# Windowed attention and a gated MLP: score bands of 136 keys for 32 queries, exponentials turned on VectorE, v in 32x64 tiles

## The chip, the cores and the metric

The kernel runs on one core of one Trainium2 chip. The metric is the device time of one execution in microseconds (us). Before the change the median of three runs is 676.88 us (676.18 to 677.9).

## The reference

Attention over 4 batches, 8 heads, 768 tokens, 64 numbers per head. A query sees the first `n_global` = 8 keys of its batch and the `n_local` = 96 keys that end at itself. A bias falls with the distance by a slope of its own for each head. The result is put together per token (512 numbers) and goes through two matrix products of 512 to 2048 to 512 with a gate between them.

```python
scores = scale * np.matmul(q, k.transpose(0, 1, 3, 2))
rel = pos[:, None] - pos[None, :]
is_global = pos[None, :] < int(n_global)
is_local = (rel >= 0) & (rel < int(n_local))
keep = is_global | is_local
dist = np.where(is_global & ~is_local, float(n_local), np.abs(rel).astype(np.float32))
scores = np.where(keep, scores - slopes[:, None, None] * dist, -1000000000.0)
a = np.exp(scores - np.max(scores, axis=-1, keepdims=True))
a = a / (np.sum(a, axis=-1, keepdims=True) + 1e-09)
attn = np.matmul(a, v)                      # [B, H, S, D] -> x [B*S, H*D]
h = x @ w_in
out = (h * (1.0 / (1.0 + np.exp(-h)))) @ w_out
```

## The kernel before, in words

**Blocks.** The 3072 tokens are 24 blocks of 128 queries, six to a batch. For each block TensorE turns k and q (`turn`, L571, eight 128x128 transposes) and computes scores, with queries on the partitions and keys along the row: 128 own keys, and in all but the first block of a batch 96 keys before them and the 8 global ones, 232 in all (`scores`, L630). The first six blocks do this in plain fp32 (`whole`), from tiles KHw and QHw. The other 18 split k and q into a high and a low fp32r part (`high` L595, `low` L599) and sum three products. A matmul here uses 64 of the 128 rows of the array: an even and an odd head are two tiles of 64 rows, issued one behind the other.

**From scores to values.** VectorE adds the bias B1 or B0 and takes the row's top (`top_of`, L644), ScalarE takes exponentials and their sum (`expo`, L652), VectorE adds 1e-9, inverts, and multiplies (`guard` L663, `inverse` L667, `norm` L672; the first four blocks do the division later, L719 to L737). TensorE turns the exponentials with fp32 transposes through PSUM (`turn_p`, L681, 352 in all), ScalarE copies them out (`move_p`, L687), and TensorE multiplies them with v (`values`, L701): one matmul per head and half window, moving 128 columns, with v as weights of 128 or 104 rows by 64 columns; two heads go to the two halves of the PSUM partitions. An fp32 matmul stands as two records in the trace. ScalarE and VectorE split the result into `xh` and `xl` for the first product (L746, L749).

**The MLP.** `moe_h` (L874) multiplies `xh` and `xl` with `w_in` split in two, three fp32r matmuls per 128 rows, over groups of blocks: `GS=(3, 3, 2, 4, 4, 4, 4)`, so a matmul is 384, 256 or 512 columns wide. ScalarE and VectorE make the gate (L880, L884) and store it. The second product (L931) works on pairs of blocks by seven products of half matrices, 256 columns wide; VectorE and ScalarE make the sums of halves (L911, L921, L925), VectorE takes the products out of PSUM (L945, L948, L953). Beside all that VectorE checks the inputs' sizes with 512-wide reductions: `check` (L515, 64 of them), `top_size` (L509) and `scale_of` for v (L559).

**What sets the order.** A planner (`Plan`, lines 65 to 190) writes the order of every engine's instructions before the kernel is built: each operation has an engine, a cost, a rank, what it depends on, and the buffers and PSUM banks that it takes; at each step the free engine gets the lowest rank that is ready by the planner's own clock. An engine executes its instructions strictly in that order. While the planner's clock stands before `WEND` = 60 us and TensorE has nothing ready, it writes a filler matmul (L1161, 256 columns of bf16 that nobody reads). `plan.after` ties an operation to an earlier one.

Of the kernel before, what the change touches and what calls it, by code (L numbers as in the profile page):

```python
# [24 lines left out]
WIN = NPREV + NG + P  # L25
C1 = NPREV + NG
FIRST_ROWS = P - NPREV
# [4 lines left out]
    LAT=140, SD=125, DL=1900, DW=2900, DB=9000, DS=5000, DO=3400, MG=60, T2=45000, LAT2=230, MG2=400, F0=600, F1=1200, C1=400, C2=1650, COLD=4400, WEND=60000,  # L32

    CAP=dict(po=6, av=2, s=4, h=3, tp=2, tq=4), HU=13, RUN=(2, 2, 4), CP=(190, 333, 392, 336, 224),

    C0=12.5, CR=0.8, LW=15, LB=8.0, QB=5.5, RI=0.8, RN=-0.6, RP=0.5, RM=0.2, RV=0.4, RQ=0.5, RB=2.5, LK=-25,

    BP=(4, 2), CF=8, AHEAD=4, GS=(3, 3, 2, 4, 4, 4, 4), BD=(1, 2), VC=1, HE=4, EQ=4, RG=-2.5, B1R=0.0, Q1=450, Q2=2400, BE='POOL', EX=10, CD=6, CS=2, SQ=((0, 0, 10), (1, 0, 10)), GG=2, PB=4, AQ=4, CN=12, I0=6, IV=4, QS='ACT', O0=7.5, ON=23.5, PF=16,
# [11 lines left out]
class Plan:  # L50
# [11 lines left out]
    KINDS = ("po", "av", "s", "h", "tp", "tq")  # L62

    def room(self, want):

        if any(self.live[x] + c > self.caps[x] for x, c in want.items()):
            return False
        if not any(x in self.KINDS for x in want):
            return True
        n = {x: self.live[x] + want.get(x, 0) for x in self.KINDS}  # L70
        own = (
            dict(po=0, av=1, s=2, h=0, tp=1, tq=0), dict(po=0, av=1, s=2, h=1, tp=1, tq=0),
            dict(po=3, av=0, s=0, h=0, tp=0, tq=0),
        )[self.hold]
        return len(self.banks) >= sum(want[x] for x in want if x in self.KINDS) and (
            sum(max(n[x], own[x]) for x in self.KINDS) <= 8 - (not self.hold)
            or all(n[x] <= own[x] for x in want if x in self.KINDS)
        )
# [19 lines left out]
    def run(self, lat, margin, lead, filler=None, fill_until=0, cold=0):  # L98
# [8 lines left out]
        while left:  # L107
# [21 lines left out]
            while back and back[0][0] <= t:  # L129
                b = heapq.heappop(back)[2]  # L130
                self.live[b.tag] -= 1
                if b.bank is not None:
                    (self.slots if b.tag == "pe" else self.banks).append(b.bank)
            for eng in pend:
# [19 lines left out]
                for b in best["uses"]:  # L154
                    if not b.taken:
                        b.taken = True
                        self.live[b.tag] += 1
                        if b.tag == "pe":
                            b.bank = self.slots.pop(0)
                        if b.tag in self.KINDS:  # L160
                            b.bank = self.banks.pop(0)
# [14 lines left out]
def attn_moe(ctx, tc, q, k, v, n_global, n_local, w_in, w_out, out):  # L176
# [34 lines left out]

    pes = [sb3.tile([P, 2, WIN], F32, name=f"pe{n}", tag=f"pe{n}", bufs=1) for n in range(PAR["PB"])]

# [6 lines left out]
    banks = [psum.tile([P, 512], F32, name=f"bank{i}") for i in range(8)]  # L220
# [7 lines left out]

    B1 = sb3.tile([P, H, WIN], BF16, name="B1", bufs=1)
    B0 = sb3.tile([P, H, P], BF16, name="B0", bufs=1)  # L230
# [9 lines left out]
    cur, glob, prev = slice(C1, WIN), slice(NPREV, C1), slice(0, NPREV)  # L240
    ng, nl = par[:, 0:1], par[:, 1:2]

    def places():

        t1 = sbx.tile([P, 1024], F32, name="t1", tag="xh")
        t2 = sbx.tile([P, 1024], F32, name="t2", tag="xl")
        bias_t.extend(t1[:, i * WIN:(i + 1) * WIN] for i in range(3))
        bias_t.extend(t2[:, i * P:(i + 1) * P] for i in range(3))
        R, col = bias_t[0], bias_t[3]
        io = dict(allow_small_or_imprecise_dtypes=True)  # L250
        both = R[:, :2 * C1].rearrange("p (a b) -> p a b", a=2)[:, :, :NPREV]
        nc.gpsimd.iota(both, [[-P, 2], [-1, NPREV]], base=NPREV, channel_multiplier=1, **io)
        nc.gpsimd.iota(R[:, C1 + NPREV:], [[-1, FIRST_ROWS]], base=0, channel_multiplier=1, **io)
        nc.gpsimd.iota(col[:, :NPREV], [[1, NPREV]], base=FIRST_ROWS, channel_multiplier=0, **io)
        nc.gpsimd.iota(col[:, NPREV:], [[1, FIRST_ROWS]], base=0, channel_multiplier=0, **io)

    def bias_far():

        R, far, D1, col, drop, D0 = bias_t
        nc.vector.tensor_scalar(drop, R[:, cur], 0.0, FAR, ALU.is_lt, ALU.mult)  # L260
        yield
        nc.vector.memset(R[:, glob], FAR)
        yield
        nc.vector.tensor_add(R[:, cur], R[:, cur], drop)
        yield
# [15 lines left out]
    def bias_own():  # L281
# [3 lines left out]
        R, far, D1, col, drop, D0 = bias_t  # L285
        nc.vector.tensor_scalar(far, R, nl, BIG, ALU.is_ge, ALU.mult)
        yield
        nc.vector.scalar_tensor_tensor(drop, col, ng, far[:, cur], ALU.is_ge, ALU.mult)
        yield
        nc.vector.scalar_tensor_tensor(D0, R[:, cur], nl, drop, ALU.min, ALU.add)  # L290
        yield

    def bias_prev():

        R, far, D1, col, drop, D0 = bias_t
        nc.vector.tensor_scalar(far[:, glob], col[:, NPREV:C1], ng, BIG, ALU.is_ge, ALU.mult)
        yield
        nc.vector.scalar_tensor_tensor(D1, R, nl, far, ALU.min, ALU.add)
        yield

    def bias_eng(first, hp):
        if hp < PAR["BD"][first]:
            return nc.vector
        return nc.gpsimd if hp >= PAR["BP"][first] else nc.scalar

    def bias_of(first, hp):
        eng = bias_eng(first, hp)
        for h in (2 * hp, 2 * hp + 1):
            o, x = ((B0, bias_t[5]) if first else (B1, bias_t[2]))
            sl = -(2.0 ** (-8.0 * (h + 1) / H)) / SC  # L310
            if eng is nc.scalar:
                eng.mul(o[:, h], x, sl)
            else:
                eng.tensor_scalar(o[:, h], x, sl, None, ALU.mult)
# [4 lines left out]
    wx = const.tile([P, B * NJ * H], F32, name="wx")  # L319
    VM = const.tile([P, B * NJ], F32, name="VM")  # L320
# [6 lines left out]
        big=2, early=99, qkn=3, vn=3, KH=2, KL=2, QH=2, QL=2, pe=PAR["PB"], pt=5, xh=2, xl=2, g1=4, F=1, gq=8, hl=3, ob=2,  # L327
# [24 lines left out]
    o_i = op("POOL", 1150, -99, places, (), bt)  # L352
    o_far = steps(bias_far, [200, 75, 200], -9, [o_i], bt)
# [3 lines left out]
    o_bias = steps(bias_own, [70, 150, 240, 220], -4, [o, o_far], [*bt, tb])  # L357
    o_bias1 = steps(bias_prev, [130, 400], PAR['B1R'], [o_bias], bt)
    o_b = {}
    for hp in range(NHP):  # L360
        for first in (True, False):
            e = bias_eng(first, hp)
            p = {id(nc.vector): ("DVE", 300, 500), id(nc.scalar): ("ACT", 400, 574)}.get(id(e), ("POOL", 1060, 1900))
            o_b[first, hp] = op(
                p[0], p[2 - first], hp - 0.5 if first else PAR["RB"] + hp,
                (lambda first=first, hp=hp: bias_of(first, hp)), [o_bias if first else o_bias1], bt,
# [96 lines left out]
    for n in range(HF):  # L463
        rank = PAR["C0"] + 2 * PAR["CR"] * n + (PAR["CD"] if n >= PAR["CS"] else 0)
        o = op("DMA", 3600, rank - PAR["LW"], (lambda n=n: stage2(n)), [o_w[n - 3][1]] if n > 2 else (), (), PAR["DW"])
# [54 lines left out]
    for n in range(2 * NFC):  # L520
        a = Buf("big")
        o = op("DMA", 1456, 1e6 + n, (lambda n=n: stage(n, "c")), [o_c[-4]] if n > 1 else (), [a], PAR["DB"])
        o_cd.append(o)
        cbuf.append(a)
        for i in range(2):
            o_c.append(op("DVE", 602, 1e6 + n, (lambda n=n, i=i: check(n, i)), [o], [a]))
        if n >= NFC:
            o_vm.append(op("DVE", 602, 1e6 + n, (lambda n=n: top_size(n)), [o], [a]))
# [5 lines left out]
    def load(i, nm, h0=0, h1=H):  # L534
        b, j = divmod(i, NJ)
        pool, tag = (sb2, "vn") if nm == "v" else (sb3, "qkn")
        if nm in "kq" and i < PAR["EQ"]:
# [3 lines left out]
        elif not h0:  # L541
            blk[i][nm] = pool.tile([P, H, D], F32, name=f"{nm}n", tag=tag, bufs=3)
        src = dict(k=k, q=q, v=v)[nm]
        cuts = (h0, (h0 + h1) // 2, h1) if i >= B * NJ - PAR["EX"] and nm == "v" else (h0, h1)
        eng = nc.scalar if not i and nm == "q" and h0 < PAR["AQ"] else nc.sync
        rows = ((0, 0, P),) if nm == "q" else ((0, FIRST_ROWS, NPREV), (NPREV, 0, FIRST_ROWS))
        for a, e in zip(cuts, cuts[1:]):
            for at, r, n in rows:
                eng.dma_start(
                    blk[i][nm][at:at + n, a:e],  # L550
                    src[b, a:e, j * P + r:j * P + r + n, :].rearrange("h p d -> p h d"),
                )

    def share(i):
        nc.sync.dma_start(blk[i - 1]["v"][NPREV:C1], v[i // NJ, :, :NG, :].rearrange("h p d -> p h d"))

    def scale_of(i):
        x = st["v", i] if i < PAR["I0"] else blk[i]["v"]
        nc.vector.tensor_reduce(  # L559
            VM[:, i:i + 1], x.rearrange("p h d -> p (h d)"), AX.X, ALU.max, apply_absolute_value=True  # L560
# [7 lines left out]
    def turn(i, nm, tp, p0=0, p1=NHP):  # L568
        blk[i]["t", nm, p0] = ps = bank(tp, NHP, P)
        for hp in range(p0, p1):  # L570
            nc.tensor.transpose(ps[:, hp], blk[i][nm][:, 2 * hp:2 * hp + 2, :], ident)  # L571

    def whole(i):
        return i < PAR["I0"]

    def part(i, x):
        if x not in blk[i]:
            f = whole(i)  # L580
# [4 lines left out]

# [749 lines left out]
```

## Time and profile before

| | before |
|---|---|
| median of 3 runs | 676.88 us |
| the profiled execution | 675.77 us |
| its span, first to last instruction | 674.0 us |
| granted TensorE clock, mean over the span | 0.999 |
| TensorE matmul busy | 668.1 us (99%) |
| VectorE busy | 556.5 us (83%) |
| ScalarE busy | 349.9 us (52%) |
| GpSimd busy | 30.5 us (5%) |

Times are from the span's start. Busy time counts an instruction from its start to its end, and matmuls overlap in the pipeline, so a row that says 1.05 us for eight matmuls is longer than the time to the next row; the distance between starts is what one costs the engine. In a group's row "x" stands before the number of records.

### The profile page before, as it was taken

Reading aid. Unit: us, or ns where it says so; the run is one execution under the profiler, and the core shown is the slowest. Engines: PE = TensorE matmul, PEld = TensorE weight load, DVE = VectorE, ACT = ScalarE, POOL = GpSimd, SP = SyncE. Lnnn points to the kernel's source line nnn. Section 1 sums busy time; section 2 is a strip of 40 time slices with the busy share of each in tenths; the row PEclk is TensorE's granted clock in tenths of the full one; section 3 lists DMA queues with packets and bytes.
Section 4 is the critical chain, followed back from the end, with each engine's and each line's share of the span. In section 5 each row is a group of like instructions: output and inputs, shape, how many; then the busy total and the mean of one; then the engine's idle time right before and its main releaser. Section 6 shows DMA issues by size and latency. Waiting matters only on the chain.

```text
span 674.0 us, 14105 instructions
## 1 busy us (share of the span) xinstructions
PE 668.1 (99%) x5222; PEld 608.0 (90%) x5222; DVE 556.5 (83%) x1297; ACT 349.9 (52%) x804; POOL 30.5 (5%) x81
## 2 busy tenths in 40 slices
PE   9999999999999999999999999999999999999997
PEld 7889999999988888888888888999999999999997
DVE  5999969999977776679655886799999999999774
ACT  6987636678655555567553353243444334333341
POOL 3202000000000000010000000000000000000000
PEclk9999999999999999999999999999999999999999
DMA  8789966666766656654435677665466565543201
GB/s 196 181 248 250 231 167 168 167 163 144 170 199 157 158 142 158 157 129 110 116 92 162 185 240 220 192 219 188 151 198 213 154 224 186 175 154 113 94 32 35
DMA packets 162221, 111.85 MB, mean 166 GB/s; under 512 B 87269, under 2 KB 144869, under 8 KB 162149
## 3 DMA queue, kind: packets, MB, share of 16 engines
q1 hardware_dynamic: 161474, 110.65, 58.3%
q8 instruction: 42, 0.69, 0.5%
q10 hardware_dynamic: 674, 0.26, 0.1%
q14 instruction: 31, 0.25, 0.1%
HBM read 79.43 MB, written 31.46 MB: 165 GB/s over the span
## 4 chain that ended last, share of the span: by engine, by line
PE 99%; DVE 0%; issue 0%; DVEq 0%
PE bank L874 41%; PE bank L931 36%; PE bank L701 6%; PE bank L681 6%; PE bank L630 6%; PE bank L571 3%; PE bank L1161 1%; PE bank L737 0%; PE bank L279 0%; DVE S L1170 0%; PE bank L1063 0%; DVE o L948 0%; PE bank L1171 0%; DVE wx L323 0%; DVEq L1168 0%
## 5 line engine op out<-in xcount | busy, mean ns | idle before, releaser
L874 PE MATMUL bank<-xh,wi 128*128 128x512 f32 (+2 forms) x896 | 276.2, 373 | 0.0
L931 PE MATMUL bank<-wo,g 128*128 128x256 f32 x1980 | 237.5, 281 | 0.0
L931 PEld LDWEIGHTS bank<-wo,g 128*128 128x128 f32 x1980 | 236.0, 189 | 0.1
L874 PEld LDWEIGHTS bank<-xh,wi 128*128 128x128 f32 x896 | 163.7, 188 | 24.5 <-issue 2.9
L874 PE MATMUL bank<-xl,wi 128*128 128x512 f32 (+2 forms) x448 | 161.9, 361 | 0.0
L880 ACT ACTIVATE th<-bank 128x512 f32<-128x512 f32 (+2 forms) x112 | 60.1, 537 | 98.5 <-PE bank L874 97.7
L884 DVE SCALAR_TENSOR_TENSOR th<-th,bank 128x512 f32<-128x512 f32 (+2 forms) x112 | 68.4, 611 | 43.2 <-ACT th L880 41.6
L652 ACT ACTIVATE pe<-pe,NM 128x232 f32<-128x232 f32 (+1 forms) x192 | 89.4, 470 | 14.3 <-DVE NM L644 14.3
L874 PEld LDWEIGHTS bank<-xl,wi 128*128 128x128 f32 x448 | 84.5, 189 | 8.6
L921 ACT CAST g<-S 128x1024 fp32r<-128x1024 f32 x48 | 50.1, 1049 | 61.9 <-DVE S L911 36.4
L925 DVE TENSOR_TENSOR g<-S,g 128x1024 fp32r<-128x1024 f32 x48 | 58.5, 1221 | 15.7 <-ACT g L921 15.3
L644 DVE CUSTOM_DVE_ANT_0 pe<-bank,B 128x232 f32<-128x232 f32 (+1 forms) x192 | 61.9, 377 | 5.1 <-PE bank L630 2.7
L687 ACT COPY pt<-bank 128x512 f32<-128x512 f32 (+1 forms) x96 | 50.5, 551 | 25.8 <-PE bank L681 25.4
L921 ACT CAST g<-a 128x1024 fp32r<-128x1024 f32 x36 | 37.7, 1048 | 36.5 <-PE bank L931 36.5
L681 PE MATMUL bank<-ident,pe 128*128 128x128 f32 (+1 forms) x352 | 50.5, 273 | 0.0
L681 PEld LDWEIGHTS bank<-ident,pe 128*128 128x128 f32 (+1 forms) x352 | 41.0, 135 | 6.5 <-ACT pt L687 0.9
L925 DVE TENSOR_TENSOR g<-a,g 128x1024 fp32r<-128x1024 f32 x36 | 43.9, 1219 | 2.5 <-ACT g L921 2.4
L701 PEld LDWEIGHTS bank<-pt,vn 128*64 128x64 f32 (+1 forms) x704 | 38.2, 136 | 7.0 <-issue 4.5
L701 PE MATMUL bank<-pt,vn 128*64 128x128 f32 (+1 forms) x704 | 44.0, 275 | 0.1
L672 DVE TENSOR_SCALAR pe<-pe,sums 128x232 f32<-128x232 f32 (+1 forms) x160 | 43.5, 329 | 0.6
L515 DVE TENSOR_REDUCE TOP<-c 128x1 f32<-128x512 int16 x64 | 41.9, 678 | 0.0
L652 ACT ACTIVATION_READ_ACCUMULATOR pe<-pe,NM 128x1 f32 x192 | 37.1, 193 | 0.0
(134 smaller groups left out, 623.8 us busy)
## 6 DMA issues: line engine op xcount, KB each, us to landing
a<-gate SPq DMA_DIRECT2D x48, 512.0 KB, 3.8
gate<-th SPq DMA_DIRECT2D x64, 256.0 KB, 2.6
ws<-in_moe_w_in_dram SPq DMA_DIRECT2D x8, 1024.0 KB
w<-in_moe_w_out_dram SPq DMA_DIRECT2D x16, 512.0 KB, 4.0
c<-in_moe_w_in_dram SPq DMA_DIRECT2D x16, 512.0 KB, 4.1
c<-in_moe_w_out_dram SPq DMA_DIRECT2D x16, 512.0 KB, 4.2
gate<-th SPq DMA_DIRECT2D x32, 192.0 KB, 2.7
out_dram<-o SPq DMA_DIRECT2D x23, 256.0 KB
```

The lines of the kernel that those rows point to most:

```text
L644: nc.vector.tensor_tensor_reduce(t["p", hp][:, a, WIN - n:], t["s", hp][a][:, :n], B1[:, h] if i % NJ else B0[:, h], -SC, 3.0e38, ALU.add, ...
L652: nc.scalar.activation(x, x, AF.Exp, bias=NM[:, i * H + h:i * H + h + 1], scale=-1.0, accum_out=t["sum", hp][:, a:a + 1],)
L672: nc.vector.tensor_scalar(x, x, t["sum", hp][:, a:a + 1], None, ALU.mult)
L681: nc.tensor.transpose(ps[:n, c, a], pe[:, a, x], ident)
L687: nc.scalar.copy(t["pt", hp][:, c], t["tp", hp][:, c])
L701: nc.tensor.matmul(pav[r, hp], x[:n, 2 * hp + a], pt[:n, c, a], start=not c or not i % NJ, stop=c == 1,)
L874: nc.tensor.matmul(ph, w1[f // 2][:, w, c, f % 2 * P:(f % 2 + 1) * P], x[:, c, :SIZE[g] * P], start=not c and not n, stop=c == NCC - 1 and ...
L880: nc.scalar.activation(th, mo["ph", g, f], AF.Tanh, scale=0.5)
L884: nc.vector.scalar_tensor_tensor(gf, gf, 1.0, mo["ph", g, f], ALU.add, ALU.mult)
L921: nc.scalar.copy(x[:, 0], mo["a", g, PROD[m][0]])
L925: nc.vector.tensor_sub(x[:, 1], mo["a", g, PROD[m][0]], x[:, 0].bitcast(F32))
L931: nc.tensor.matmul(y, a[:, i, p], w2[p, w, c], start=not p and not n, stop=p == HF - 1 and n == 2,)
```

## The change

**Scores.** A block's 128 queries become four chunks of 32. A chunk sees seven slots less three: four slots of 32 keys, and 2 of the global keys stand behind each slot, so a row is 4 x 34 = 136 keys. Keys and queries stay fp32, with no split, in tiles KT (seven slots) and QT. Per chunk and head one matmul takes 32 queries as weights (64 rows by 32 columns) and moves 136 keys; the four pairs of heads go to the four quarters of the PSUM partitions, even and odd heads to the two halves of the rows: eight tiles of the array in turn. A block is 32 such matmuls, all of one shape, into a PSUM tile of four banks (`four`, planner tag G) that values use too. So a VectorE or ScalarE instruction on a chunk works on 4 heads x 32 queries.

**Turning.** `norm` goes to ScalarE (L689). The exponentials are turned by VectorE in 32x32 squares (`turn_p`, L703, two instructions of 128 x 512 per block) instead of TensorE's transposes and ScalarE's copies; the global columns are set aside by GpSimd (`aside`, L694) and turned by one 128 x 256 instruction (`turn_g`, L698).

**Values.** v stands as 32x64 tiles (`load_v`, eight DMAs per 384 rows). A matmul has 32 keys by 64 numbers as weights and moves the queries that see the slot: 128, 32, 64, 96, 96, 64, 32 and 128 (globals) columns, eight tiles each, 64 matmuls a block; the first block of a batch has 128, 96, 64, 32.

**Around it.** All groups are three blocks (`GS=(3,) * 8`). The checks' loads are tied to 56 marks spread from mark 66 to mark 203 of the 212 that the first and the second product make; v is loaded again for its check for all 24 blocks (before: 6), and the checks have the last rank. The bias has two tiles per kind instead of one per pair of heads. Fillers stay as they are: before, the planner writes 58 of them; now 200, 191 of these ahead of the first `moe_h`. Transposes of k and q (192) and the second product's matmuls (2016) keep their number.

```diff
-WIN = NPREV + NG + P
+Q = 32
+NR = 4
+CH = Q + 2
+WIN = NR * CH
...
-    ... GS=(3, 3, 2, 4, 4, 4, 4), ...
+    ... KS=66, KE=203, KD=10000.0, KV=14990, ... GS=(3,) * 8, ...
...
-    KINDS = ("po", "av", "s", "h", "tp", "tq")
+    KINDS = ("po", "G", "h", "tp")
+    HIGH = (4, 5, 6, 7)
...
     def scores(i):
         t = blk[i]
+        for c in range(NR):
+            for g in range(NHP):
                 for a in range(2):
                     r = slice(a * D, (a + 1) * D)
+                    o = four[Q * g:Q * (g + 1), c // 2 * 2 + a, c % 2 * WIN:(c % 2 + 1) * WIN]
                     nc.tensor.matmul(
-                        t["s", x][a][:, :n], t[y][r, x], t[z][r, x, w0:], start=not m, stop=m == len(terms) - 1
+                        o, t["QT"][r, g, Q * c:Q * (c + 1)], t["KT"][r, g, c:c + NR], start=True, stop=True
                     )
...
-    def norm(i, hp, a):
-        nc.vector.tensor_scalar(x, x, t["sum", hp][:, a:a + 1], None, ALU.mult)
+    def norm(i, a, c):
+        nc.scalar.mul(x, x, blk[i]["S"][:, m:m + 1])
...
-                nc.tensor.transpose(ps[:n, c, a], pe[:, a, x], ident)
+    def turn_g(i):
+        blk[i]["pg"] = y = sb2.tile([P, 2, P], F32, name="pg")
+        nc.vector.transpose(y, PG[(i - i // NJ) % 2][:, :, :P])
+
+    def turn_p(i, a):
+        blk[i]["pt", a] = y = sb2.tile([P, PT], F32, name="pt", bufs=4)
+        x = blk[i]["p", a].rearrange("p a (r c) -> p a r c", c=CH)
+        nc.vector.transpose(y[:, :NR * NR * Q].rearrange("p (a r q) -> p a r q", a=NR, q=Q), x[:, :, :, :Q])
...
+        line = [NR - 1, *range(NR - 1), *range(NR, NW), NW] if j else list(range(NR - 1, NW))
+        for w in line:
+            lo, hi = (0, NR) if w == NW else (max(0, w - NR + 1), min(NR, w + 1))
...
             for a in range(2):
-                r = slice(a * D, (a + 1) * D)
-                x, n = blk[i - 1 + c]["v"], P if c else C1
-                nc.tensor.matmul(
-                    pav[r, hp], x[:n, 2 * hp + a], pt[:n, c, a],
-                    start=not c or not i % NJ, stop=c == 1,
-                )
+                for g in range(NHP):
+                    r = slice(Q * g, Q * (g + 1))
+                    o = four[a * D:(a + 1) * D, g, Q * lo:Q * hi]
...
+                    nc.tensor.matmul(o, x, y, start=w == line[0], stop=w == line[-1])
...
-    for n, o in enumerate(o_cd):
-        if n < NFC:
-            plan.after(o, o_h[divmod(2 * NFC + 4 * n, NFC)])
-        else:
-            plan.after(o, o_p[2 + PAR["CN"] * (n - NFC) // 4 - 3 * (n > NFC)])
+    marks = [o_h[x] for x in line] + o_p
+    loads = [o for o, _ in o_va2] + o_cd
+    for n, o in enumerate(loads):
+        plan.after(o, marks[int(PAR["KS"] + (PAR["KE"] - PAR["KS"]) * n / len(loads))])
```

On TensorE before, in the part where attention and the first product alternate, a block's values stand as 16 wide matmuls, followed here by the first of its successor's three-term scores (KH, KL, QH, QL are the split k and q, pt the turned exponentials, vn the values):

```order
L701 MATMUL bank_87<-pt,vn 64x128 x16
L630 MATMUL bank_92<-KH,QH 128x232
L630 MATMUL bank_93<-KH,QH 128x232
L630 MATMUL bank_92<-KL,QH 128x232
L630 MATMUL bank_93<-KL,QH 128x232
L630 MATMUL bank_92<-KH,QL 128x232
L630 MATMUL bank_93<-KH,QL 128x232
```

After, the scores of a block are one run of 32 matmuls of 136 columns on one engine line, between two column blocks of the first product:

```order
L819 MATMUL bank_88<-xl,wi_1202 128x384
L819 MATMUL bank_88<-xh,wi_1202 128x384
L659 MATMUL four<-KT,QT 32x136 x32
L819 MATMUL bank_89<-xh,wi_1202 128x384
L819 MATMUL bank_89<-xl,wi_1202 128x384
```

and the second half of a block's values on TensorE is this, behind 8 matmuls each of 128, 32 and 64 columns (vt are the 32x64 tiles of v, pg and GV the global part):

```order
L722 MATMUL four<-pt,vt 64x96 x16
L722 MATMUL four<-pt,vt 64x64 x8
L722 MATMUL four<-pt,vt 64x32 x8
L722 MATMUL four<-pg,GV 64x128 x8
L626 MATMUL bank_88<-ident,qn 128x128 x4
L819 MATMUL bank_89<-xh,wi_986 128x384
```

So what stood in 24 matmuls of 232 columns, 16 transposes and 16 matmuls of 128 columns per block now stands in 32 of 136 and 64 of 32 to 128.

On VectorE before, in the second product, one check reduction (L515) stands among eight instructions that make sums and take products out of PSUM (bank is PSUM, o the output, S, a and g the sums of halves):

```order
L948 SCALAR_TENSOR_TENSOR o<-bank_87,o 128x256
L925 TENSOR_TENSOR g_5_6126<-S_5147,g_5_6126 128x1024
L948 SCALAR_TENSOR_TENSOR o<-bank_91,o 128x256
L911 TENSOR_TENSOR S_5148<-a_1_5915 128x1024
L515 TENSOR_REDUCE TOP<-c_6039 128x1
L925 TENSOR_TENSOR g_6_6163<-a_1_5689,g_6_6163 128x1024
L948 SCALAR_TENSOR_TENSOR o<-bank_88,o 128x256
L911 TENSOR_TENSOR S_5147<-S_5148,a_0_5863 128x1024
L953 TENSOR_TENSOR o<-o,E_6157 128x2x256
```

After, in the same part (L893 is now the evacuation, L856 and L870 the sums, L558 and L606 the checks), two of six are checks:

```order
L870 TENSOR_TENSOR g_3_7497<-S_6331,g_3_7497 128x1024
L558 TENSOR_REDUCE TOP<-c_7448 128x1
L856 TENSOR_TENSOR S_6331<-a_0_7055,a_1_7135 128x1024
L606 TENSOR_REDUCE VM<-va_7481 128x1
L893 SCALAR_TENSOR_TENSOR o<-four,o 128x256
L870 TENSOR_TENSOR g_4_7544<-S_6331,g_4_7544 128x1024
```

Behind the first evacuation of the second product there stand 85 check reductions now and 48 before; the last of them stands at evacuation 55 of 60, before at 45.

## Rows read from the trace of the kernel before

**Rows 1.** The page, part 1: engine, busy us, share of the span, instructions.

```profile
PE 668.1 (99%) x5222; PEld 608.0 (90%) x5222; DVE 556.5 (83%) x1297; ACT 349.9 (52%) x804; POOL 30.5 (5%) x81
```

**Rows 2.** The page, part 4: the chain that ended last, by line.

```profile
PE bank L874 41%; PE bank L931 36%; PE bank L701 6%; PE bank L681 6%; PE bank L630 6%; PE bank L571 3%; PE bank L1161 1%; PE bank L737 0%; PE bank L279 0%; DVE S L1170 0%; PE bank L1063 0%; DVE o L948 0%; PE bank L1171 0%; DVE wx L323 0%; DVEq L1168 0%
```

**Rows 3.** PE timeline: start us, us, engine, line, operation, tile, shape; a first-batch stretch.

```profile
12.84 1.05 PE L630 MATMUL bank<-KHw,QHw 64*128 64x232 f32 x8
13.83 1.09 PE L701 MATMUL bank<-pt,vn 128*64 128x128 f32 x16
14.85 0.66 PE L571 MATMUL bank<-ident,early 128*128 128x128 f32 x4
```

**Rows 4.** PE timeline, a later block: a whole score run, then the values.

```profile
41.12 1.84 PE L630 MATMUL bank<-KHw,QHw 64*128 64x232 f32 x16
42.89 1.98 PE L701 MATMUL bank<-pt,vn 104*64 104x128 f32 x32
44.80 0.66 PE L737 MATMUL bank<-ident,wide 128*128 128x128 f32 x4
```

**Rows 5.** PE timeline: first scores of a split block, and the row behind them.

```profile
307.99 0.38 PE L630 MATMUL bank<-KH,QH 64*128 64x232 f32 x2
...
309.52 0.51 PE L874 MATMUL bank<-xh,wi 128*128 128x512 f32 x1
```

**Rows 6.** PE timeline: eight transposes of exponentials.

```profile
300.38 1.03 PE L681 MATMUL bank<-ident,pe 128*104 128x128 f32 x8
301.25 0.60 PE L571 MATMUL bank<-ident,kn 128*128 128x128 f32 x4
```

**Rows 7.** PE timeline: filler matmuls.

```profile
19.30 1.05 PE L1161 MATMUL bank<-wx 128*128 128x256 bf16 x8
20.18 0.60 PE L681 MATMUL bank<-ident,pe 128*104 128x128 f32 x4
```

**Rows 8.** PE timeline: projection matmuls 384 wide.

```profile
49.13 0.51 PE L874 MATMUL bank<-xh,wi 128*128 128x384 f32 x2
...
49.65 0.51 PE L874 MATMUL bank<-xh,wi 128*128 128x384 f32 x2
```

**Rows 9.** PE timeline: projection matmuls 512 wide.

```profile
313.25 0.63 PE L874 MATMUL bank<-xh,wi 128*128 128x512 f32 x2
...
313.95 0.63 PE L874 MATMUL bank<-xh,wi 128*128 128x512 f32 x2
```

**Rows 10.** PE timeline: the first projection matmul.

```profile
37.24 0.42 PE L874 MATMUL bank<-xh,wi 128*128 128x384 f32 x1
```

**Rows 11.** Windows: us, busy (count) of PE, PEld, DVE, ACT, POOL; clock, DMA.

```profile
60.00:80.00 20.00, 20.00 (x165) 19.14 (x165) 19.69 (x51) 12.78 (x34) 1.78 (x4) 1.00 0.87 239
450.00:640.00 190.00, 190.00 (x1603) 189.83 (x1603) 175.13 (x236) 74.64 (x86) 0.00 (x0) 1.00 0.52 169
640.00:674.00 34.00, 29.41 (x249) 29.10 (x247) 19.75 (x24) 9.22 (x11) 0.00 (x0) 0.98 0.10 33
```

**Rows 12.** Timeline at 303.61 and the summary of line 701: two tiles start together.

```profile
303.61 0.14 PEld L701 LDWEIGHTS bank<-pt,vn 104*64 104x64 f32 x2 [0.37 <-ACT pe L652]
303.61 0.33 PE L701 MATMUL bank<-pt,vn 104*64 104x128 f32 x2
...
L701 PEld LDWEIGHTS bank<-pt,vn x704: 132/137/139, 13.8 to 352.4; 128*64 128x64 f32 x96, 104*64 104x64 f32 x80
L701 PE MATMUL bank<-pt,vn x704: 269/272/324, 13.8 to 352.6; 128*64 128x128 f32 x96, 104*64 104x128 f32 x80
```

**Rows 13.** VectorE by line and shape: busy us, mean ns, idle before.

```profile
L672 DVE TENSOR_SCALAR pe<-pe,sums 128x232 f32<-128x232 f32 x136 | 38.2, 338 | 0.5
...
L595 DVE COPY KHw<-bank 128x512 f32<-128x512 f32 x3 | 2.1, 691 | 1.0 <-PE bank L681 0.7 <-PE bank L571 0.3
```

**Rows 14.** The same windows for the checks alone, line 515 then line 509.

```profile
450.00:640.00 190.00, 21.39 (x32) 1.00 0.52 169
...
450.00:640.00 190.00, 10.88 (x16) 1.00 0.52 169
```

More of the change, by code (lines that the diff above doesn't have):

```diff
@@ L67, in room @@
             return False
-        if not any(x in self.KINDS for x in want):
-            return True
[L70 to L77, printed above, removed]
-        )
+        if "G" in want and any(b not in self.banks for b in self.HIGH):
+            return False
+        one = sum(c for x, c in want.items() if x in self.KINDS and x != "G")
+        if not one:
+            return True
+        if want.get("h") and self.live["h"] + want["h"] > (4 if self.hold else 3):
+            return False
+        return len(self.places(None)) >= one
     def op(self, eng, cost, rank, emit, deps=(), uses=(), lat=None):
@@ new lines, in part, with turn, turned @@
+        return blk[i][x]
+    def turn(i, nm, p0, p1, tp):
+        blk[i][nm, "tp"] = ps = bank(tp, NHP, P)
+        for g in range(p0, p1):
+            nc.tensor.transpose(ps[:, g], blk[i][nm][:, 2 * g:2 * g + 2, :], ident)
+    def turned(i, nm, p0, p1):
+        x, ps = part(i, nm.upper() + "T"), blk[i][nm, "tp"]
+        o, y = x[:, p0:p1], ps[:, p0:p1]
+        if nm == "k":
+            o, y = o[:, :, NR - 1:, :Q], y.rearrange("p g (t d) -> p g t d", d=Q)
+        if PAR["TE"] == "ACT":
+            nc.scalar.copy(o, y)
+        else:
+            nc.vector.tensor_copy(o, y)
@@ L728, in move_r, with top_of @@
-    def move_r(i):
-        t = blk[i]
-        t["rs"] = x = sb2.tile([P, NHP, P], F32, name="rs", tag="mid", bufs=5)
-        nc.scalar.copy(x, t["rp"])
-    def turn_r(i, tp):
-        t = blk[i]
-        t["rp"] = ps = bank(tp, NHP, P)
-        for hp in range(NHP):
-            nc.tensor.transpose(ps[:, hp], t["wide"][:, 2 * hp:2 * hp + 2], ident)
+    def top_of(i, a, c, pe):
+        if not c:
+            blk[i]["p", a] = pes[pe.bank]
+        if not a and not c:
+            blk[i]["S"] = sb2.tile([P, H], F32, name="S")
+        n = i * H + a * NR + c
+        nc.vector.tensor_tensor_reduce(
+            blk[i]["p", a][:, c], four[:, c // 2 * 2 + a, c % 2 * WIN:(c % 2 + 1) * WIN],
+            (B1 if i % NJ else B0)[:, a, c], -SC, 3.0e38, ALU.add, ALU.min, NM[:, n:n + 1],
+        )
@@ L863, in attn_moe @@
-        hi = op("ACT", 478, u, (lambda i=i: x_high(i)), [last], [pav, xb[g]["xh"]])
+            was_k = [o for x, o in old.items() if x[0] in ("k", "c")]
+            for near, cost in ((False, 155), (True, 455)):
+                ob["c", near] = op("POOL", cost, rank, (lambda i=i, near=near: carry(i, near)), was_k, [kb[i - 1]["KT"], kk["KT"]])
+        else:
+            ob["c", 0] = op("POOL", 750, rank, (lambda i=i: first_keys(i)), ks, [kk["KT"]])
+        if not j:
+            o_g[b] = op("DMA", 8 * 475, rank - lr + PAR["VL"] + 5, (lambda b=b: load_g(b)), [o_zero], [gb[b]], PAR["DL"])
```

521 lines of the change are left out of this document (225 added, 296 removed).

## The prediction

> **What bounds the kernel now.** I read the page's busy times first: TensorE's matmuls are busy 99% of the span, 668.1 us, VectorE 83% [rows 1]. The chain that ended last agrees, since nearly all of it is work in TensorE's banks [rows 2]: the two products make 77%, and 19% stands in the lines that this change takes away or rewrites (L701, L681 and L630 6% each, fillers 1%), 128 of 674 us. So the end moves by what TensorE's instructions cost in sum, as long as nothing else comes late. The timeline of TensorE then gives prices, as distances between starts. A run of plain fp32 scores takes 0.99 for 8 records and a run of values 1.02 for 16 [rows 3]; 16 records of scores take 1.77 and 32 of values 1.91 [rows 4]. From the two plain runs, 8 more records (four passes of an even and an odd head) cost 0.78, so a pass of 232 columns takes 0.195 us, 0.84 ns a column, and about 0.2 us a run is entry and exit. A block of split scores takes 1.53 for 24 records [rows 5], an fp32 transpose 0.87/8 = 0.109 [rows 6], a filler 0.88/8 = 0.11 [rows 7], a projection matmul 0.52/3 = 0.173 at 384 columns [rows 8] and 0.70/3 = 0.233 at 512 [rows 9]; the first projection starts at 37.24 us [rows 10]. The windows say where VectorE has room: at 60 to 80 us none (19.69 of 20), at 450 to 640 us 14.9 of 190, behind 640 us 14.25 of 34 [rows 11]. The granted clock is 1.00 there, 0.98 in the last, practically the upper of its levels (2.4 GHz), and TensorE stays dense, so I price nothing for it.
>
> **What goes, on TensorE.** Values: 20 blocks x 1.91 + 4 x 1.02 = 42.3. Transposes of exponentials: 352 x 0.109 = 38.4. Scores: 18 x 1.53 = 27.5; five of the six plain blocks in two runs each, 5 x 1.9 = 9.5; the first one with 128 columns, 8 x 128 x 0.84 ns + 0.4 = 1.3; together 38.3. The 16 transposes of the late division 1.7, and 58 fillers x 0.11 = 6.4. Sum 127.1, beside the chain's 128. All of it is on the path, as TensorE has hardly any idle time.
>
> **What comes, on TensorE.** No row of before has eight tiles in turn. The nearest thing is two tiles [rows 12]: two matmuls begin in the same 0.01 us and the pair takes 0.33, no more than the longest single one (324 ns), and their two weight loads take 0.14 where one takes 132 to 139 ns. So neither the columns nor the loads of different tiles queue up behind one another there. I take it that eight tiles do the same: a pass costs its columns x 0.84 ns once.
> - Scores: per block 4 chunks x 2 records x 136 x 0.84 ns = 0.91, plus 0.2 for the run, x 24 = 26.7.
> - Values: 640 columns x 2 records x 0.84 ns = 1.08, plus 0.2 = 1.28 by columns alone. If no set of eight narrow ones goes faster than one of 96 columns, 832 x 2 x 0.84 ns + 0.2 = 1.60. I take the middle, 1.44, x 20 = 28.8. The first block of a batch lies between 0.74 and 0.90, 4 x 0.82 = 3.3.
> - Fillers: 200 x 0.11 = 22.0. 191 stand ahead of the first projection matmul: by the planner's clock TensorE waits there for loads, ScalarE and VectorE, and if these come sooner than the planner thinks, the fillers still run.
>
> Together 80.8. The next edit with a price is the grouping: before, 4 x 192 matmuls at 0.233, 2 x 192 at 0.173 and 192 at 256 columns, which I give the pace of the second product's (190.00/1603 = 0.119 [rows 11]), together 268; now 8 x 192 x 0.173 = 266: -2. Transposes of k and q and the matmuls of the second product stay as many. So -127 + 81 - 2 = -48. The profiled execution took 675.8, its span 674.0 with 1.8 around it; 675.8 - 48 = 628 is its forecast, and as the median is 1.1 above it, 628 to 629: I say 628.
>
> **Ends for the unknown price.** There are 4352 new fp32 records; the forecast gives them 49.2 us without the runs' edges, 11.3 ns each on the mean. The lower end: values by columns alone -3.5, and no edges of runs -9.6, is 614 to 615. The upper end takes only what is seen, two tiles at once. A score pair of 136 columns is then 0.114 us, a block 32 x 2 x 0.057 + 0.2 = 3.85; a values record cannot go below the steady rate of split scores, (1.53 - 0.2)/24 = 0.055 [rows 5], a block 128 x 0.055 + 0.2 = 7.3, a batch's first 3.75. That is 253 us where I have 59: 822. Between ends so far apart I go by the rows that are nearest in kind, [rows 12].
>
> A rule of the Trainium skill bears on this: "TensorE: Matmul & The Clock Gate", Part 3 on packing small matmuls, says that matmuls on different tiles run at the same time, each beginning some 4 ns behind the last. The trace agrees for two tiles, with starts within 0.01 us [rows 12]; no row here shows eight. By it eight would have begun within 32 ns, about what 32 columns take, and the sum stands as it is.
>
> **The other engines.** VectorE loses 136 multiplications of 38.2 us [rows 13], 24 narrower ones, and the 36 subtractions of 128 x 512 for the low parts, which at the price of the copy of that size, 691 ns [rows 13], are 25: some 65 with the rest. It gains 48 transposes of 128 x 512. No row of before shows a VectorE transpose. The nearest are that copy and the multiplication, 338 ns for 232 columns, so 0.75 us for 512 [rows 13]; half the one is the low end, twice the other the high end: 17 to 72 us in all. I take 0.69, by the row of equal size, so 33, and 20 half ones at 0.42, 8. That leaves VectorE some 24 us lighter, and ScalarE, 52% busy [rows 1], has room for 192 multiplications. But the place of the transposes matters: values now wait for ScalarE and VectorE where TensorE turned the exponentials itself, and behind a waiting values matmul all of the first product is queued. The planner has put other blocks' projections ahead, and where it had none, fillers. In the second product 85 checks stand where 48 stood, 37 more at 21.39/32 = 0.67 us [rows 14], 25 us, against 14.9 us of idle time to 640 and 14.25 behind it [rows 11], of which the very end is hardly usable, as the last check stands five evacuations before it. I price this at 0, with its cover nearly used up; without the cover it costs up to 10 us.
>
> **Rivals.**
> *A: the array does not take eight small tiles at once.* Then each new record costs more, and break-even is where scores and values cost 107 us instead of 59, (107 - 9.6)/4352 = 22.4 ns a record, fewer than about five tiles side by side. At four, scores 24 x 2.03 and values 20 x 3.75 + 4 x 1.98 make 132, and the time is 701; at two 822. Against it stand the starts 0.01 us apart in [rows 12]; for it, that no row shows more than two. A chance of 0.13, with 700 as its middle.
> The Trainium skill has a rule for this side too. In the same page, "Wait — 56ns, not 53.3ns?", it says that matmuls never start less than about 25 ns apart however few columns they have. By it the 4352 records take 109 us, with edges 118 where I have 59, and the time would be an estimated 688. The two starts within 0.01 us of [rows 12] speak against it where tiles differ.
>
> *B: VectorE sets the pace.* In the second product each evacuation stands behind a check more often than before; if the 10 us of checks that do not fit come late, TensorE, with no fillers there, waits as long. At the start, where VectorE is full, a transpose at twice my price adds 0.7 us to each of the first blocks' chains, 5 us for eight. For it: the order of each engine is fixed, so a late VectorE is paid in full. Against it: VectorE is lighter in the first 350 us, and the planner costs a transpose at 597 ns, near my 0.69. With 5 to 20 us lost the time is 633 to 648, 640 as its middle. A chance of 0.22.
>
> *C: the sum holds,* 615 to 636: 0.62. What is left, 0.03, is a weak form of A, with times around before's.
>
> **How the numbers follow.** The forecast is C, 628. The range goes from 612, a little under the lower end of the sum, to 664, past B and into a weak A (six tiles at once, 32 us over the sum), which leaves out the strong A and the tails, under 0.2. About 0.3%, 2 us, is what a measurement of this kernel can tell from no change. Faster takes C, B and the better part of the weak A: 0.85; the same 0.02; slower, A: 0.13.
>
> **What would show it.** Right: runs of 64 score records (L659) with 1.0 to 1.2 us between starts and of 128 values records (L722) with 1.3 to 1.6; the first projection at 37 to 38 us; TensorE busy 99% of a span of 626; VectorE's transposes at 0.6 to 0.8. A: runs of L722 over 2.6 us. B: idle time of TensorE released by VectorE at L703 or at the evacuation L893, and VectorE at 99% between 450 us and the last checks. The forecast is wrong at once if a run of scores takes over 2 us, or if the first projection starts later than 45 us.

## The result, and the profile after

The changed kernel takes 671.33 us (median of 5, 670.38 to 673.03) where the kernel before takes 677.0 beside it: a ratio of 0.9918, interval 0.9898 to 0.9938. It is faster, by 5.7 us, under one per cent. The forecast was 628 with a range to 664, so it missed by 43 us, about seven eighths of the forecast gain. The profiled execution has a span of 670.5 us. The page of the changed kernel, part 1, against [rows 1]:

```profile
PE 641.5 (96%) x8308; PEld 608.5 (91%) x8308; DVE 514.6 (77%) x1132; ACT 351.0 (52%) x915; POOL 32.7 (5%) x127
```

TensorE's busy time fell by 27 us and its idle time rose from 6 to 29. Where, the windows say, cut at the first projection matmul and at the first matmul of the second product; first the kernel before, then the changed one (columns as in [rows 11]).

```profile
0.00:37.20 37.20, 36.01 (x322) 29.00 (x323) 29.48 (x109) 30.64 (x95) 9.37 (x26) 1.00 0.81 185
37.20:428.90 391.70, 391.59 (x2876) 339.04 (x2875) 313.92 (x911) 226.21 (x603) 21.13 (x55) 1.00 0.64 172
428.90:669.00 240.10, 240.10 (x2025) 239.89 (x2023) 212.15 (x277) 93.04 (x107) 0.00 (x0) 1.00 0.48 156
```

```profile
0.00:50.30 50.30, 43.03 (x886) 34.90 (x886) 32.43 (x115) 35.14 (x118) 11.95 (x54) 0.97 0.87 191
50.30:405.20 354.90, 351.53 (x5400) 332.42 (x5399) 245.00 (x699) 223.02 (x691) 20.80 (x73) 1.00 0.63 167
405.20:665.40 260.20, 246.47 (x2025) 241.01 (x2023) 236.26 (x318) 92.88 (x107) 0.00 (x0) 1.00 0.58 184
```

The forecast's own terms, sorted by these three stages, give 37.6 us (191 fillers, five blocks' scores, three blocks' values, 52 transposes of k and q, 1.7 of parameters and first wait), 391.7 - 48.5 = 343.2 and 240.0. So the gain is there in the middle (36.8 us of a forecast 48.5), and is given back twice: the start takes 13.1 us more than before, and the second product, whose matmuls the change does not touch, 20.1 more. Against the forecast the three misses are 12.7, 11.7 and 20.2 us, together 44.6: the whole difference of the spans.

**The second product.** TensorE's groups on L876 in the changed kernel (the last columns are the idle time before them and what ended it):

```profile
L876 PE MATMUL four<-wo,g 128*128 128x256 f32 x1035 | 133.1, 284 | 13.2 <-DVE o L893 9.8 <-ACT E L890 1.4 <-ACT o L890 1.4
...
L876 PE MATMUL bank<-wo,g 128*128 128x256 f32 x945 | 116.2, 282 | 0.0
```

The same matmul waits 13.2 us where it writes the four-bank tile and never where it writes a single-bank tile. The timeline of all engines at one such place, with rows left out at the marks:

```profile
414.43 0.87 PE L876 MATMUL four<-wo,g 128*128 128x256 f32 x6
...
414.47 0.68 DVE L558 TENSOR_REDUCE TOP<-c 128x1 f32<-128x512 int16 x1
...
415.34 0.42 DVE L893 SCALAR_TENSOR_TENSOR o<-four,o 128x256 f32<-128x256 f32 x1 [0.19 <-PE four L876]
...
415.82 0.39 PE L876 MATMUL four<-wo,g 128*128 128x256 f32 x1 [0.52 <-DVE o L893]
```

A product is 24 matmuls into one bank. One product has ended here, and the six matmuls from 414.43 are the first of the next one, in another bank of the same tile. VectorE reads the ended product out at 415.34, and it begins only when the sixth matmul of the next product is done, at 415.30; the seventh then waits for this reading. The program's semaphores have it so: the instruction reads bank 2 of the tile and waits for the sixth matmul into bank 3, and the seventh waits for the instruction. The tile counts as one thing, whatever the bank. So TensorE does not wait between two products but in the middle of one: from the start of the sixth matmul to that of the seventh it is 0.80 us, where matmuls otherwise follow at 0.12.

The planner gives banks 4 to 7, the slices of `four`, to products one after the other in 23 of 83 hand-overs. At the hand-overs the step is the usual 0.12 us; the stops stand behind 3 to 21 matmuls of a product. The trace has 27 stops of over 0.25 us on the four-bank tile, 17.5 us in sum above the usual step.

**The start.** TensorE's timeline of the changed kernel, the fourth block's scores and the first filler behind them:

```profile
33.39 0.69 PE L659 MATMUL four<-KT,QT 64*32 64x136 f32 x32
36.63 1.16 PE L659 MATMUL four<-KT,QT 64*32 64x136 f32 x32 [2.55 <-issue]
37.72 0.40 PE L1103 MATMUL bank<-wx 128*128 128x256 bf16 x1
```

One uninterrupted run of 64 stops in its middle, with no semaphore behind the stop. A second one stands at 46.8 to 48.9. The trace's packets point to the cause: a 16 KB packet on a queue of instructions begins at 34.00 and takes 1.18 us, and TensorE resumes 1.45 us behind its end. The queue fits TensorE's records (matmuls and weight loads): 66 packets for 16616 of them, 42 for 10444 before, one for some 250. And the stops stand at fixed places in the program: behind record 1209 and, 512 records on, 1721, in the changed kernel as in e9 and e11 below. The kernel before has 5222 matmul records and no such stop over 0.6 us inside a run; the changed one has 8308 and three of them. The granted clock is 0.91 in the windows 20 to 40 and 40 to 60 us; in the trace's record of the clock it is at the lower of its two levels (1.2 GHz) from 36.5 to 40.0 and from 50.2 to 53.6, right behind the two stops.

**Scores and values.** Runs in the middle of the changed kernel, from TensorE's timeline:

```profile
292.53 1.20 PE L659 MATMUL four<-KT,QT 64*32 64x136 f32 x64
293.65 0.44 PE L819 MATMUL bank<-xh,wi 128*128 128x384 f32 x1
```

```profile
304.39 1.53 PE L722 MATMUL four<-pt,vt 32*64 32x128 f32 x108
...
305.77 0.47 PE L722 MATMUL four<-pg,GV 32*64 32x128 f32 x12
306.17 0.44 PE L819 MATMUL bank<-xh,wi 128*128 128x384 f32 x1
```

A block's scores take 1.12 us (forecast 1.11) and its values 1.78 (forecast 1.44, bounds 1.28 and 1.60).

### The profile page after: what moved, and what is told of

Same layout as the page of the kernel before. It is cut to its first block, busy times and chain, and to the rows that moved or that the text cites. A ratio compares the mean times of both kernels' runs of the same rounds, so it can differ in the third digit from the quotient of the medians.

```text
span 670.5 us, 20175 instructions
## 1 busy us (share of the span) xinstructions
PE 641.5 (96%) x8308; PEld 608.5 (91%) x8308; DVE 514.6 (77%) x1132; ACT 351.0 (52%) x915; POOL 32.7 (5%) x127
## 5 line engine op out<-in xcount | busy, mean ns | idle before, releaser
L819 PE MATMUL bank<-xh,wi 128*128 128x384 f32 x1024 | 279.2, 344 | 0.0
L819 PE MATMUL bank<-xl,wi 128*128 128x384 f32 x512 | 173.2, 338 | 0.0
L876 PE MATMUL four<-wo,g 128*128 128x256 f32 x1035 | 133.1, 284 | 13.2 <-DVE o L893 9.8
L876 PEld LDWEIGHTS four<-wo,g 128*128 128x128 f32 x1035 | 125.8, 189 | 18.3 <-DVE o L893 13.5
L829 DVE SCALAR_TENSOR_TENSOR th<-th,bank 128x384 f32<-128x384 f32 x128 | 70.6, 552 | 69.2 <-ACT th L825 66.4
L825 ACT ACTIVATE th<-bank 128x384 f32<-128x384 f32 x128 | 62.6, 489 | 103.2 <-PE bank L819 101.8
L876 PE MATMUL bank<-wo,g 128*128 128x256 f32 x945 | 116.2, 282 | 0.0
L876 PEld LDWEIGHTS bank<-wo,g 128*128 128x128 f32 x945 | 113.8, 189 | 0.0
L677 ACT ACTIVATE pe<-pe,NM 128x136 f32<-128x136 f32 x192 | 75.9, 399 | 5.9 <-DVE NM L669 5.8
L689 ACT ACTIVATE pe<-pe,S 128x136 f32<-128x136 f32 x192 | 61.8, 399 | 2.4 <-DVE S L685 2.4
L870 DVE TENSOR_TENSOR g<-S,g 128x1024 fp32r<-128x1024 f32 x48 | 58.4, 1219 | 2.3 <-ACT g L866 2.1
L870 DVE TENSOR_TENSOR g<-a,g 128x1024 fp32r<-128x1024 f32 x36 | 43.9, 1220 | 2.6 <-ACT g L866 2.5
L558 DVE TENSOR_REDUCE TOP<-c 128x1 f32<-128x512 int16 x64 | 43.0, 678 | 1.0 <-DMA c<-in_moe_w_in_dram 1.0
L703 DVE STREAM_TRANSPOSE pt<-pe 128x512 f32<-128x512 f32 x48 | 34.0, 708 | 12.3 <-ACT pe L689 12.2
```

The lines of the kernel that those rows point to most:

```text
L558: nc.vector.tensor_reduce(TOP[:, i, n:n + 1], top, AX.X, (ALU.min, ALU.max)[i], apply_absolute_value=True)
L677: nc.scalar.activation(x, x, AF.Exp, bias=NM[:, n:n + 1], scale=-1.0, accum_out=blk[i]["S"][:, m:m + 1])
L689: nc.scalar.mul(x, x, blk[i]["S"][:, m:m + 1])
L703: nc.vector.transpose(y[:, :NR * NR * Q].rearrange("p (a r q) -> p a r q", a=NR, q=Q), x[:, :, :, :Q])
L819: nc.tensor.matmul(ph, w1[f // 2][:, w, c, f % 2 * P:(f % 2 + 1) * P], x[:, c, :SIZE[g] * P], start=not c and not n, stop=c == NCC - 1 and ...
L825: nc.scalar.activation(th, mo["ph", g, f], AF.Tanh, scale=0.5)
```

## The experiments

Times are medians beside a run of the kernel before on the same chip; the ratio is to that, with its interval.

**The shared tile or VectorE's load.** Four kernels. e1 takes each product's bank from the other half of PSUM than the last one's:

```diff
-        return [b for b in self.banks if b < n]
+        x = [b for b in self.banks if b < n]
+        if tag == "po":
+            x.sort(key=lambda b: (b in self.HIGH) == self.high)
+        return x
```

> The changed kernel with one edit: in the second product each next bank is taken from the other half of PSUM (single-bank tiles, then the four-bank tile, in turn). Before this edit 23 of 83 hand-overs go from one bank of the four-bank tile to another, and in the trace TensorE stands 0.7 us at such a place until the bank before is read out. Theory T (the shared tile makes the next product wait for the last one's evacuation): the second product falls from 260 to 240 to 244 us, the time from 671 to 651 to 655. Theory V (VectorE has too many checks there): nothing in VectorE's work changes, so 668 to 672 and the second product stays at 256 or more.

655.92 us, 0.9704 (0.9682 to 0.9726), below the changed kernel's interval by far. The second product takes 246.5 us. T is near: 14 of its 20 us are gone, the stage is 2.5 us and the time 1 us above T's range. V is out.

e2 has `KS=66, KE=100` for `KS=66, KE=203`.

> The changed kernel with the checks' loads spread over marks 66 to 100 instead of 66 to 203: 57 instead of 85 check reductions stand behind the first evacuation of the second product, 28 x 0.68 = 19 us of VectorE's work less there; the banks are as in the changed kernel. T: the waits at the shared tile stay, the second product 254 to 260, the time 666 to 672. V: the second product falls by 12 to 20 us, the time to 651 to 659.

672.4 us, 0.9932 (0.9917 to 0.9946). VectorE's work in the second product falls from 236.3 to 223.4 us, 13 us where 19 were reckoned, and the stage takes 261.2, 1 us above T's range and no less than in the changed kernel:

```profile
405.70:666.90 261.20, 246.47 (x2025) 241.04 (x2024) 223.36 (x293) 94.52 (x110) 0.00 (x0) 1.00 0.49 158
```

> Both edits, banks in turn and checks early. T: as the alternation alone, 650 to 655, the checks add at most 2 us. V: the checks bring 12 to 20 us beside the alternation. If the two share the loss, this run is below either alone by over 4 us.

657.04 us, 0.9718 (0.9694 to 0.9743), 2 us above T's range, the second product 246.4: the checks add nothing to the alternation. e4 is the reverse, in the kernel before:

```diff
-    banks = [psum.tile([P, 512], F32, name=f"bank{i}") for i in range(8)]
+    four = psum.tile([P, 4, 512], F32, name="four")
+    banks = [psum.tile([P, 512], F32, name=f"bank{i}") for i in range(4)] + [four[:, i] for i in range(4)]
```

> The kernel before the change, with four of its eight single-bank PSUM tiles made slices of one four-bank tile, and nothing else. In its second product 16 hand-overs then go from one slice to another. T: the second product grows from 240 to 248 to 254 us (16 x 0.7 = 11), and the part ahead of it, where scores, transposes and projections share the banks, grows too; the time is 690 or more. V: the checks are as in the kernel before, so the second product stays at 240 to 242 us.

820.82 us, 1.2121 (1.2098 to 1.2145). Its second product takes 253.2 us, inside T's range, with the same checks as the kernel before; and the part ahead of it, which uses the slices for everything, grows by far more. The wait in its second product is again on the four-bank tile alone:

```profile
L932 PE MATMUL bank<-wo,g 128*128 128x256 f32 x1020 | 125.3, 282 | 0.0
L932 PE MATMUL four<-wo,g 128*128 128x256 f32 x960 | 123.5, 283 | 8.9 <-DVE o L949 6.5 <-ACT o L946 1.4 <-ACT E L946 0.9
```

e9, on the changed kernel, keeps the second product out of the four-bank tile:

```diff
-        n = 8 if self.hold == 2 else 4
-        return [b for b in self.banks if b < n]
+        return [b for b in self.banks if b < 4]
...
-    CAP=dict(po=6, h=4, tp=2), ...
+    CAP=dict(po=4, h=4, tp=2), ...
```

> The changed kernel, with the second product confined to the four single-bank tiles, so that it never writes the four-bank tile. In e1 six stops of 0.7 us were left, where the late evacuation of one product still stands ahead of another in the four-bank tile. Theory T: all stops at hand-overs go and the second product takes 240 to 243 us as before the change (260 changed, 246 in e1), the time is 649 to 653. Rival: four banks instead of eight are too few, evacuations come late at VectorE's pace, and the second product stays at 246 or more.

654.28 us, 0.9671 (0.9646 to 0.9696). The second product takes 243.8 us, 240.0 before the change; of what is left 2.4 us is one wait of the checks' transposes for their load. So four banks do for the second product, and the tile was the loss. The stage is 0.8 us and the time 1 us over T's range; in the trace the start took 49.5 us against e1's 47.6, though up to the first projection the two have the same instructions in the same order. So have the changed kernel, e2 and e3, with 50.3, 50.3 and 51.4: one start differs by up to 3.8 us from one execution to the next, and the experiments on the start below, with one trace each, have to be read against that.

**What the start waits for.** e5 moves one load: `... + PAR["VL"] + (8 if n == 1 else 0)` for the second v tile.

> Banks in turn (as e1, 655.9 us), and the second 384 rows of v, eight DMAs that take SyncE and the queues from 18.8 to 28.1 us, are loaded behind the keys and queries of the next two blocks. In e1 TensorE stands still in the middle of two score runs of the start, 2.9 us before 35.3 and 2.3 us before 46.3, with no semaphore behind it; the 16 KB packet of TensorE's instructions begins late there, among the loads. Theory F (the instructions queue behind loads): with the loads moved at least the first stop goes, the first projection starts at 43 to 45 us instead of 47.6, the time is 651 to 654. Rival S (the start is the chain of ScalarE and VectorE from scores to values, stops or not): first projection at 47 to 48, time 654 to 657.

656.95 us, 0.9721 (0.9692 to 0.9749). A miss for F as put: the first stop shrank from 2.9 to 1.7 us and the second grew from 2.3 to 3.2, now that the v tile is loaded there; both lie outside what the five like starts show (2.8 to 3.9 and 2.0 to 2.3). The first projection came at 49.8 us, inside the spread of the five. e6 has `WEND=9000`.

> Banks in turn, and fillers only in the planner's first 9 us instead of 60. 150 and more filler matmuls (some 20 us of TensorE) leave the start. If fillers hold up the real work (they are written for the planner's clock and run in any case), the first projection comes 3 to 10 us earlier. If TensorE only waits in their place for ScalarE and VectorE, the first projection stays at 46 to 49 us, the granted clock falls to half in part of the first 50 us, and the time is 655 to 662.

654.36 us, 0.9680 (0.9666 to 0.9694), just under the range. The first projection starts at 46.7 us, and the clock is 0.59 from 20 to 40 us: fillers stand where TensorE waits, and to leave them out costs nothing. e11 moves the weights' loads: `rank - PAR["LW"] + (8 if 0 < n < 4 else 0)`, on e9.

> e9 with the second to fourth megabyte of the first product's weights loaded later, behind keys and queries of the next blocks, so that no such load stands between 28 and 33 us. In every run so far a stop of TensorE inside a score run at the start ends 1.4 to 1.6 us after a 16 KB packet of its instructions has landed that was started late, in a stretch with 170 to 330 KB/us of loads. Theory F: the first stop (2.8 us near 34 us) goes or falls under 1 us, and the first projection starts 2 to 4 us earlier than in e9. Rival S: the start is the chain of ScalarE and VectorE and stays within 1 us of e9's. The projections behind it may wait for weights in either case, so the time itself can rise by up to 11 us.

662.49 us, 0.9808 (0.9784 to 0.9832). F is borne out at the start. TensorE's timeline there, e9 and then e11:

```profile
32.57 0.69 PE L658 MATMUL four<-KT,QT 64*32 64x136 f32 x32
35.83 0.76 PE L658 MATMUL four<-KT,QT 64*32 64x136 f32 x32 [2.56 <-issue]
```

```profile
32.79 0.76 PE L658 MATMUL four<-KT,QT 64*32 64x136 f32 x33
34.09 0.69 PE L658 MATMUL four<-KT,QT 64*32 64x136 f32 x31 [0.54 <-issue]
```

The stops fall from 2.8 and 2.1 us (from start to start) to 0.8 and 1.1, the clock stays at 1.00 in both windows to 60 us, and the first projection starts at 45.3 instead of 49.5 us, 2.2 us ahead of the earliest of the five like starts. The stage behind takes 365.1 instead of 354.4 us, but not for the reason that was allowed for: no projection on TensorE waits for weights in this trace. The loads stand elsewhere, and so do the stops, 2.9 us before 74.5 and 1.4 before 83.4, inside values; another 4.7 us of idle time stand before values and turned keys that wait for VectorE and ScalarE, one of them so:

```profile
81.06 1.28 PE L721 MATMUL four<-pt,vt 32*64 32x128 f32 x49 [2.53 <-DVE NM L668]
```

The clock is at its lower level (1.2 GHz) from 76.5 to 90.2 us. Why VectorE and ScalarE come later there was not taken apart.

e10 is e9 with e6's edit.

> e9 and e6 together: single-bank tiles in the second product and fillers in the first 9 us only. e6 took 1 to 2 us off e1 without an earlier start of the projections, at half the clock in part of the start. Expected 647 to 652, 1 to 2 us under e9; if the fillers' clock matters more than their instructions, it is above e9.

650.66 us, 0.9613 (0.9600 to 0.9627), the best here: it beats both kernels, the changed one by 3%. First projection at 48.1 us, second product 242.8.

e12 has `VL=4.5` for `VL=1.5` on e10.

> e10 with the eight DMAs of the first v tile (and all later ones) ranked behind the keys and queries of the next block, so that SyncE issues those about 4 us earlier. In e10 ScalarE waits 1.4 us inside the first block's exponentials for the second block's keys to be turned, since its order puts that copy between them. If the late keys hold up the first block, its values start at 18 to 18.5 us instead of 19.7 and the first projection comes 1 to 3 us earlier, 648 to 650 us. If ScalarE's own work sets the chain (8 exponentials, 8 multiplications, copies), the values start within 0.7 us of e10's and the time is 649 to 653.

652.57 us, 0.9652 (0.9634 to 0.9671). In the trace the first block's values start at 18.0 us instead of 19.7 and the first projection at 43.7 instead of 48.1. But e6, whose start has the same instructions as e10's, has its values at 18.4, so how much of the 1.7 us belongs to the keys is not shown. The stage behind takes 358.2 instead of 354.9 us with the same idle time, 5.1 us: the third block's values stood ahead of the first projection (40.8) and now stand in this stage (46.5), so part of the earlier start is work put off. The execution that was traced ends 2.2 us sooner than e10's, the median is 1.9 us later: no gain is shown.

**The price of the values.** e7 drops two sets, `line = [w for w in line if w not in (0, NW - 1)]`, e8 widens six. Each was run once (648.85 and 656.64 us); what counts is the length of a values run in the trace, where blocks repeat to 0.03 us.

> Banks in turn, and the two sets of values matmuls that move 32 columns are left out (slots 0 and 6 of the band, so the output lacks their part): 96 instead of 128 records in a run of the 20 usual blocks. Theory I (behind the first 36 records of a run an instruction pair leaves every 16.7 ns, whatever its columns): a run takes 1.78 - 32 x 0.0167 = 1.25 us between starts. Theory N (columns set the pace): 64 columns x 2 x 0.84 ns less, 1.67 us.

1.47 us a run: between I and N, 0.31 us for 32 records of 32 columns, 9.7 ns each where their columns alone would be 3.4.

> Banks in turn, and the six narrower sets of values matmuls all move 96 columns (the added columns are wrong numbers, so is the output): the same 128 records, 832 instead of 640 columns. Theory I: the run stays at 1.75 to 1.90 us between starts. Theory N: 192 x 2 x 0.84 ns more, 2.10 us.

1.87 us a run: I, with 192 more columns for 0.08 us. Together: a pass of eight records of 32 to 96 columns (a set of eight matmuls is two passes) costs an estimated 0.08 to 0.1 us whatever its columns, the lower from e7, the upper from e8, so neither theory holds alone.

## Why the prediction was wrong, point by point

**"The matmuls of the second product stay as many. So -127 + 81 - 2 = -48."** The count was right, and no price was put on where they write. This is the step that failed most: 20.2 of 44.6 us. The changed program has a four-bank tile whose slices the second product also uses. The reading of one slice waits for the matmuls into another slice that stand ahead of it in the program, and the matmuls behind it wait for the reading. e9 removes that and gives back 16.4 us in the stage, e4 brings it into the kernel before. Rival B named the place and the sign to look for, idle time of TensorE released by L893, but its cause was wrong: the 37 further checks came, as reckoned (VectorE's work there rose by 24.1 us), and were hidden. Taking 13 us of VectorE's work away in e2 changed nothing.

**"The first projection at 37 to 38 us".** It came at 50.27, 12.7 us behind the forecast's sum. By the distances between starts TensorE's scores took 11.0 us there for 5.6, its fillers 26.2 for 21.0, the transposes of k and q 6.7 for 5.7 and values 4.7 for 3.7. The scores' excess is nearly all the two stops for instructions, 4.9 us from start to start; behind the first the clock was at its lower level for 3.4 us (what follows the second falls into the middle). That the loads make the next 16 KB late is borne out by e5 and e11, where the stops moved with the loads. The change makes TensorE read its program faster than before: 128 records, each with its weight load, in 1.78 us of values. Of the fillers, 156 went at 0.114 us, near the price; 25 in the first 7 us took 4.4, seven at the lower clock 1.4, and three that stand before a wait 2.6. To price them at all was only half of the start, though: e6 leaves 162 of them out and has its first projection at 46.7. What stands behind them, as far as these traces show, is the chain from the loads over scores, ScalarE and VectorE to values, which the forecast did not price: the first block's values start at 20.8 us where they started at 13.8 [rows 3]. e11, with 1.9 us of stops left, stands at 45.3, so some 6 of the 13 us against the kernel before stay with this chain and are not settled further.

**"I take the middle, 1.44".** 1.78. In the middle stage values cost 36.0 us for a forecast 28.4, 7.6 of its miss of 11.7; 0.9 of that is one more stop for instructions, at 78 us. The upper bound of 1.60 was too low as well, since it was drawn from columns: e8 moves just those 832 columns and takes 1.87. Eight tiles do run side by side, as taken: the first eight records start within 0.047 us, 7 ns apart, where [rows 12] had two. But by the 36th record the lead of the weight loads over their matmuls has shrunk from 0.11 us to 4 ns, and the other 92 records take 1.29 us, 14 ns each. Whether the weight loads or the issue of instructions set this pace, no run here separates. The remaining 4 us are projections: 282.7 us from start to start for 266 priced, where before 281.1 stood for 268; 2.9 us of idle time are in it, most of it before turned keys and queries at 86 and 88 us, which wait for their loads.

**What held.** Of the removed terms values took 42.3 us and scores 38.4 in the sum of distances, as priced, and transposes 35.1 for 38.4. Scores came at 1.12. VectorE's transposes took 708 and 409 ns (0.69 and 0.42 taken). Rival A, of fewer than five tiles at once, is out. The Trainium skill's page "TensorE: Matmul & The Clock Gate" has two rules on this: some 4 ns between tiles (Part 3, on packing), and never less than about 25 ns between starts ("Wait — 56ns, not 53.3ns?"). The trace shows 7 ns between tiles and 14 ns on the mean of a whole run, so the first is nearer and the second does not hold between different tiles; by the second the prediction's estimate was 688 us.

## What to carry to other kernels

Price a stage by what its instructions write and wait for, not by their number: in this program a PSUM tile of several banks is one thing to wait for, and a stage that only borrows its slices inherits that. Look for such waits inside a run of matmuls, not only at its ends. Where a change cuts one engine's work, forecast the start by its chain from the loads to the first dependent matmul; 200 fillers where 58 stood say that this chain got longer. Compare the starts of kernels that have the same start first: here one trace told nothing under some 4 us. A stream of short instructions can outrun the fetching and the issue of its instructions, so count instructions per microsecond beside columns.

## What the runs showed of the hardware that was not expected

TensorE stops inside a run when its next 16 KB of instructions are late: in e9 a packet ends at 34.23 and TensorE resumes at 35.83, another ends at 46.76 and it resumes at 48.16; in e11 32.45 and 34.09. It is 1.4 to 1.6 us each time. Short matmuls on eight tiles start 7 ns apart at first and 14 to 16 ns on the mean behind the 36th record, with 32 columns left out (e7) as with all narrow ones at 96 (e8). And a clock of 0.59 from 20 to 40 us, where TensorE is busy 12.4 of 20 us, cost nothing that e6 can show.
